# Routing of the last block: eight tiles in the first slot table, one operation at a time over slots 1 to 6, logits in plain float32

## The chip, the core and the metric

The kernel runs on one core of a Trainium2 chip. The metric is the time on the device in microseconds (us), the median of a few runs. The engines meant here are TensorE (PE in the rows, its weight loads PEld), VectorE (DVE), ScalarE (ACT), GpSimd (POOL) and SyncE (SP), which issues most transfers. Each engine works through its own queue in order.

## What is computed

Three stages follow each other: windowed attention, a dense layer with a leaky activation, and a layer of eight experts in which each token goes to the one expert with the largest logit.

```python
# attention: batch 4, 8 heads, 576 tokens, head size 64, causal window of 64
attn = softmax(where(mask, q @ k.T / 8, -1e9)) @ v          # 2304 tokens x 512
h = attn @ w_in                                            # 512 x 2048
x = (maximum(h, 0) + alpha * minimum(h, 0)) @ w_out        # 2304 x 512
logits = x @ w_gate                                        # 512 x 8
expert_idx = argmax(logits, axis=1)
gate_w = softmax(logits)[arange(N), expert_idx]
for e in range(8):                                         # w1: 512 x 1024, w2: 1024 x 512
    mask = expert_idx == e
    out[mask] = gate_w[mask, None] * (maximum(x[mask] @ w1[e], 0) @ w2[e])
```

Large products run as three products of rounded halves ("fp32r"): high by high, low by high and high by low. The high half is a rounded copy, made on ScalarE; the low half is the rest, made by a subtraction on VectorE. Weights and activations are both split in this way.

## The kernel before

The 2,304 tokens are 18 tiles of 128 and five blocks of 4, 4, 4, 3 and 3 tiles. Attention and dense layer run block by block. The routing of a block begins when its dense output (`stage`) is there: logits, then `r_gate` (largest logit, the softmax weight, the one-hot of the expert), `r_rank` (nine small matmuls that count the tokens of each expert before each token), `r_place` (row and column of each token in a list of 128 x 152 entries, eight experts by tiles of 128), `r_onehot` (two one-hot matrices A and B for each tile), `r_list` (a matmul of A by B) and `r_add` (their sum into the list `lst`). For the first three blocks the logits are VectorE dot products (`r_dot`), also for the fourth. For the last block they go over TensorE: `r_trans` transposes a tile of `stage` and splits it into halves (a copy on ScalarE, a subtraction on VectorE, L454 and L455), and `r_logits` multiplies both halves by the split gate weights `wgc` (eight matmuls of 16 or 8 columns, L463 and L464, then a copy of 8 columns on ScalarE and an addition on VectorE).

The expert layer runs in slots. A slot is one tile of 128 tokens of one expert. `slot_table` computes from the list which expert and which tile each slot has. The first table (part 0) is made once the first four blocks are routed; it gives `K1` slots, filled with whole tiles of the first 1,920 tokens. The second (part 1) gives the rest, after the last block's routing. Of 25 possible slots 21 run with these inputs (504 matmuls of L743, 24 in a slot).

In `slot(s)`, in the order of the code: `e1` (24 matmuls, the first expert matrix), `htr` twice (transposes of the hidden layer, with a copy on ScalarE and the subtraction L730 on VectorE), `e2mm` (24 matmuls, the second expert matrix), `xtr` (transpose of the next slot's gathered tokens, with the subtraction L703), `gather(s + 2)` (index from list and table on VectorE, L684 to L689, then an indirect transfer by GpSimd). At eight places `step(i)` puts in one split of the next slot's weights (`split2`: the copy L819 on ScalarE, the subtraction L825 on VectorE), and at the odd ones `sregs` and `reload` on SyncE, which loads the weights for slot s + 2 if its expert is another than that of the slot before (1 MB for each of four pieces).

The order inside the slots is written out by hand (`manual_schedule`): each engine gets its instructions in the order of the code. `extra` names what of the last block's routing is put ahead of the split at which step. Before, that is: in slot 0 the transposes and logits of the three tiles and `r_gate`, in slot 1 `r_rank`, `r_place` and the first one-hots, in slot 2 the list and the first part of the second table (`table_step`), in slot 3 the rest. The block before slot 0, where the last dense block and the first table overlap, is ordered by a scheduler.

Of the kernel before, what the change touches and what calls it, by code (L numbers as in the profile page):

```python
# [7 lines left out]
FP32 = mybir.dt.float32  # L8
# [9 lines left out]
NE = 8  # L18
NSLOT = 25
K1 = 6  # L20
# [60 lines left out]
def attn_moe_moe_kernel(  # L81
# [55 lines left out]
    wgc = const.tile([128, 4, 2 * NE], FP32R, name="wgc")  # L137
# [310 lines left out]
    def r_trans(j, t, tag="xs"):  # L448
        b = rbank(j).rearrange("p (k c) -> p k c", k=4)
        for k in range(4):  # L450
            PE.transpose(b[:, k, :], stage[j][:, t, k * 128:k * 128 + 128], ident)
        th = spare(tag + "h")
        tl = spare(tag + "l")
        ACT.copy(out=th, in_=b)  # L454
        DVE.tensor_tensor(out=tl, in0=b, in1=f32(th), op=ALU.subtract)  # L455
        x1t[j, t] = (th, tl)

    def r_logits(j, t):
        th, tl = x1t.pop((j, t))
        n = BLOCKS[j][1]  # L460
# [27 lines left out]
    def r_gate(j):  # L488
# [10 lines left out]
        DVE.tensor_tensor(out=ls, in0=lg, in1=mb, op=ALU.subtract)  # L499
        ACT.activation(out=ls, in_=ls, func=ACTF.Exp)  # L500
        eq = small("eq", [NE])
        DVE.tensor_tensor(out=eq, in0=lg, in1=mb, op=ALU.is_equal)
        DVE.tensor_tensor(out=eq, in0=eq, in1=desc8.unsqueeze(1).to_broadcast([128, n, NE]), op=ALU.mult)
        mx = small("mx", [])
        DVE.tensor_reduce(out=mx, in_=eq, axis=AX.X, op=ALU.max)
        oh = small("oh", [NE], BF16)
        DVE.tensor_tensor(out=oh, in0=eq, in1=mx.unsqueeze(2).to_broadcast([128, n, NE]), op=ALU.is_equal)
        ss = small("gs", [])
        DVE.tensor_reduce(out=ss, in_=ls, axis=AX.X, op=ALU.add)
        DVE.tensor_scalar(out=ss, in0=ss, scalar1=1e-9, scalar2=None, op0=ALU.add)  # L510
        DVE.reciprocal(out=stage[j][:, 0:n, 512:XW], in_=ss.unsqueeze(2).to_broadcast([128, n, XW - 512]))
        s = stage.pop(j)
# [17 lines left out]
    def r_place(j):  # L530
# [20 lines left out]
        jf = small("gs", [])
        DVE.tensor_copy(out=jf, in_=ji)
        cf = small("cf", [])
        DVE.tensor_scalar(out=cf, in0=mx, scalar1=-float(NTILE), scalar2=float(NE * NTILE), op0=ALU.mult, op1=ALU.add)
        DVE.tensor_tensor(out=cf, in0=cf, in1=jf, op=ALU.add)
        for u in range(n):
            DVE.tensor_tensor(out=ohsum, in0=ohsum, in1=oh[:, u, :], op=ALU.add)
        rc[j] = (cf, pf)

    def r_onehot(j, h=0):  # L560
# [3 lines left out]
        for t in range(2 * h, min(2 * h + 2, n)):  # L564
# [36 lines left out]
    def slot_table(part):  # L601
# [9 lines left out]
        PE.matmul(out=b[:, 0:NE], lhsT=one16, rhs=ohsum, start=True, stop=True)  # L611
        ni = small("ni", [NE], I32)
        DVE.tensor_scalar(out=ni, in0=b[:, 0:NE], scalar1=127.0 * part, scalar2=None, op0=ALU.add)
        DVE.tensor_scalar(out=ni, in0=ni, scalar1=7, scalar2=None, op0=ALU.logical_shift_right)
        nb = small("nb", [NE])
        DVE.tensor_copy(out=nb, in_=ni)
        give(("R", NB))
        yield
        if part:
            DVE.tensor_tensor(out=nb, in0=nb, in1=tab["done"], op=ALU.subtract)  # L620
# [47 lines left out]
    def table_step():  # L668
        next(gen1, None)
# [378 lines left out]
```

## Time and profile before

| what | us |
|---|---|
| median of three runs | 767.79 (767.28 to 767.81) |
| the profiled execution, its own time | 767.55 |
| its span, first to last instruction | 765.8 |
| TensorE busy in the span | 748.1 (98%) |
| VectorE busy | 609.0 (80%) |
| ScalarE busy | 456.3 (60%) |
| start of slot 0 | 485.31 |
| start of slot 1 | 505.29 |
| start of slot 5 | 560.68 |

A slot's start is the start of its first `e1` matmul. The time that a slot takes is best read as the distance between such starts; busy times say which engine fills it. A row of the timeline gives the start and the length of an instruction, or of several of one form in a row. Ends overlap with the next start, so what an operation costs its engine is the distance from its start to the next one's.

### The profile page before, as it was taken

The numbers are of one execution on the slowest core, as the hardware profiler recorded it, in microseconds if no ns is written. First come the engines' busy times: TensorE is split into PE (matmuls) and PEld (weight loads), VectorE is DVE, ScalarE is ACT, GpSimd is POOL, SyncE is SP. The second block draws the span as 40 slices with busy tenths as digits, with TensorE's granted clock in tenths as the row PEclk, the third lists the DMA queues.
The fourth block names the chain that finished last, engine by engine and source line by source line (L and its number), as shares of the span: only waits on it lengthen the run. The fifth ranks groups of instructions, "written<-read, shape, count | busy, mean of one in ns | idle before, by whom it ended". The sixth has DMA issues, their size and how long they took to land. (4 is left out here: it accounts for less than half of the span.)

```text
span 765.8 us, 12642 instructions
## 1 busy us (share of the span) xinstructions
PE 748.1 (98%) x4567; PEld 612.4 (80%) x4572; DVE 609.0 (80%) x1154; ACT 456.3 (60%) x868; POOL 89.4 (12%) x106
## 2 busy tenths in 40 slices
PE   7999999999999999999999999999999999999996
PEld 3688888888888888888888988777788888888884
DVE  4999999477556756668775956699999999999997
ACT  4887565543243342344342323778889999889986
POOL 1210001000000000000000001011222213131322
PEclk9999999999999999999999999999999999999999
DMA  9983413233032122223323116420194176757611
GB/s 347 411 363 131 157 64 120 68 103 105 24 94 97 62 62 98 62 98 90 93 66 111 56 43 268 161 109 28 56 353 169 32 279 258 290 214 258 215 73 51
DMA packets 29442, 109.90 MB, mean 144 GB/s; under 512 B 3582, under 2 KB 3966, under 8 KB 22208
## 3 DMA queue, kind: packets, MB, share of 16 engines
q1 hardware_dynamic: 25856, 98.25, 36.0%
q0 software_dynamic: 3520, 10.80, 4.3%
q8 instruction: 38, 0.62, 0.3%
q14 instruction: 28, 0.23, 0.1%
HBM read 154.09 MB, written 10.26 MB: 215 GB/s over the span
## 5 line engine op out<-in xcount | busy, mean ns | idle before, releaser
L825 DVE TENSOR_TENSOR hl<-hl,hl 128x1024 fp32r<-128x1024 f32 x176 | 211.1, 1222 | 17.7 <-ACT hl L819 17.0
L819 ACT CAST hl<-hl 128x1024 fp32r<-128x1024 f32 x176 | 180.4, 1049 | 6.0 <-DMA hl<-in_wx_dram 4.5
L743 PE MATMUL acc<-hl,xl 128*128 128x512 f32 x504 | 130.6, 400 | 2.5 <-DVE xl L730 2.5
L404 ACT ACTIVATE g<-h 128x512 f32<-128x512 f32 (+1 forms) x80 | 44.6, 558 | 141.2 <-PE h L391 110.9
L389 PE MATMUL h<-xh,hl 128*128 128x512 f32 (+1 forms) x320 | 120.6, 377 | 0.8 <-DVE g L408 0.8
L390 PE MATMUL h<-xl,hl 128*128 128x512 f32 (+1 forms) x320 | 118.1, 369 | 0.0
L391 PE MATMUL h<-xh,hl 128*128 128x512 f32 (+1 forms) x320 | 118.0, 369 | 0.0
L432 PE MATMUL acc<-hl,gl 128*128 128x512 f32 x288 | 113.2, 393 | 0.4 <-DVE gl L414 0.4
L433 PE MATMUL acc<-hl,gh 128*128 128x512 f32 x288 | 112.6, 391 | 0.0
L431 PE MATMUL acc<-hl,gh 128*128 128x512 f32 x288 | 109.9, 400 | 0.0
L743 PEld LDWEIGHTS acc<-hl,xl 128*128 128x128 f32 x504 | 91.2, 188 | 21.4 <-DVE xl L730 3.8
L408 DVE SCALAR_TENSOR_TENSOR g<-g,beta,h 128x512 f32<-128x512 f32 (+1 forms) x80 | 55.3, 691 | 56.0 <-ACT g L404 55.7
L414 DVE TENSOR_TENSOR gl<-g,gh 128x512 fp32r<-128x512 f32 (+1 forms) x80 | 50.8, 634 | 36.9 <-PE acc L432 22.2
L349 ACT CAST gh<-g 128x512 fp32r<-128x512 f32 (+1 forms) x80 | 46.5, 581 | 51.9 <-DVE g L408 50.2
L691 POOL DMA_INDIRECT gx<-x1d,ixg x23 | 39.9, 1733 | 290.3 <-DVE xh L703 166.6
L389 PEld LDWEIGHTS h<-xh,hl 128*128 128x128 f32 x320 | 60.1, 188 | 11.0 <-DVE g L408 1.3
L715 PE MATMUL h<-hl,xh 128*128 128x512 f32 x168 | 67.7, 403 | 0.0
L485 DVE SCALAR_TENSOR_TENSOR dot<-stage,wge 128x512 bf16<-128x512 f32 x96 | 65.8, 686 | 2.1 <-DMA wge<-in_wgt_dram 0.8
L390 PEld LDWEIGHTS h<-xl,hl 128*128 128x128 f32 x320 | 60.2, 188 | 8.6 <-DVE xl L377 0.5
L717 PE MATMUL h<-hl,xh 128*128 128x512 f32 x168 | 66.2, 394 | 0.4 <-DVE xh L703 0.2
L391 PEld LDWEIGHTS h<-xh,hl 128*128 128x128 f32 x320 | 60.1, 188 | 7.9
L716 PE MATMUL h<-hl,xh 128*128 128x512 f32 x168 | 65.5, 390 | 0.0
(194 smaller groups left out, 1071.8 us busy)
## 6 DMA issues: line engine op xcount, KB each, us to landing
hl<-in_wx_dram SPq DMA_DIRECT2D x92, 1024.0 KB
hl<-in_wcat_dram SPq DMA_DIRECT2D x14, 1024.0 KB
qk<-in_qkv_dram SPq DMA_DIRECT2D x30, 448.0 KB
v<-in_qkv_dram SPq DMA_DIRECT2D x30, 256.0 KB
wge<-in_wgt_dram SPq DMA_DIRECT2D x24, 256.0 KB
x1d<-stage SPq DMA_DIRECT2D x3, 1032.0 KB
hl<-in_qkv_dram SPq DMA_DIRECT2D x6, 448.0 KB
x<-in_wcat_dram SPq DMA_DIRECT2D x2, 1024.0 KB
```

The lines of the kernel that those rows point to most:

```text
L389: PE.matmul(out=h[:, 0:n], lhsT=w_in_op(f, k, 0), rhs=xh[:, k, :], start=(k == 0), stop=False)
L390: PE.matmul(out=h[:, 0:n], lhsT=w_in_op(f, k, 0), rhs=xl[:, k, :], start=False, stop=False)
L391: PE.matmul(out=h[:, 0:n], lhsT=w_in_op(f, k, 1), rhs=xh[:, k, :], start=False, stop=(k == 3))
L431: PE.matmul(out=a, lhsT=gh[:, c0:c0 + 128], rhs=w_out_op(f, 0), start=(f == 0), stop=False)
L432: PE.matmul(out=a, lhsT=gl[:, c0:c0 + 128], rhs=w_out_op(f, 0), start=False, stop=False)
L433: PE.matmul(out=a, lhsT=gh[:, c0:c0 + 128], rhs=w_out_op(f, 1), start=False, stop=(f == 15))
L485: DVE.scalar_tensor_tensor(out=o, in0=stage[j][:, t, 0:512], scalar=1.0, in1=wge[j, e], op0=ALU.mult, op1=ALU.mult, accum_out=rt[j][:, t, ...
L715: PE.matmul(out=o, lhsT=th[:, k, :], rhs=wh, start=(k == 0), stop=False)
L717: PE.matmul(out=o, lhsT=tl[:, k, :], rhs=wh, start=False, stop=(k == 3))
L743: PE.matmul(out=o, lhsT=x[:, f % 4, :], rhs=w[:, lo, (f % 2) * 512:(f % 2) * 512 + 512], start=(x is th and f == 0 and lo == 0), stop=(x i ...
L819: ACT.copy(out=t[:, 0, :], in_=r)
L825: eng.tensor_tensor(out=t[:, 1, :], in0=r, in1=f32(t[:, 0, :]), op=ALU.subtract)
```

## The change

`K1` goes from 6 to 8: the first table has eight slots, the second at most 17. The logits of the last block are computed from one plain float32 copy of the transposed tile: four float32 products of eight columns for a tile, then `r_take` copies the result; the halves, `wgc`, and the small copy and addition go. The first tile's transposes and logits stay in slot 0, those of the second and third go to slot 1. The functions of the routing become generators that yield after each VectorE operation; `route_last` strings them together with pauses of three steps ahead of what TensorE has to deliver, and `tick` takes one or two steps of it at each split from the sixth of slot 1 on (`PACE`), and one more at four places of slots 2 to 6. For the other blocks `drain` runs the same functions in one go.

```diff
-K1 = 6
+K1 = 8
@@ r_trans, r_logits
-        th = spare(tag + "h")
-        tl = spare(tag + "l")
-        ACT.copy(out=th, in_=b)
-        DVE.tensor_tensor(out=tl, in0=b, in1=f32(th), op=ALU.subtract)
-        x1t[j, t] = (th, tl)
+        x1t[j, t] = mp.tile([128, 128 * NBT], FP32, tag="g", bufs=1, name="g").rearrange("p (k c) -> p k c", k=4)
+        ACT.copy(out=x1t[j, t], in_=b)
...
-            PE.matmul(out=b[:, 0:2 * NE], lhsT=th[:, k, :], rhs=wgc[:, k, :], start=(k == 0), stop=False)
-            PE.matmul(out=b[:, 0:NE], lhsT=tl[:, k, :], rhs=wgc[:, k, 0:NE], start=False, stop=(k == 3))
-        lo = rp.tile([128, NE], FP32, tag="lo", name="lo")
-        ACT.copy(out=lo, in_=b[:, NE:2 * NE])
-        DVE.tensor_tensor(out=rt[j][:, t, :], in0=b[:, 0:NE], in1=lo, op=ALU.add)
+            PE.matmul(out=b[:, 0:NE], lhsT=x[:, k, :], rhs=wg[:, k * NE:k * NE + NE], start=(k == 0), stop=(k == 3))
+        x1t[j, t] = b
+
+    def r_take(j, t):
+        DVE.tensor_copy(out=rt[j][:, t, :], in_=x1t.pop((j, t))[:, 0:NE])
@@ r_gate, r_place, r_onehot, slot_table: after each VectorE operation
+        yield
...
+    WAIT = 3
...
+    def route_last():
+        j = NB - 1
+        yield from r_gate(j)
+        yield from pause()
+        r_rank(j)
+        yield from pause()
+        yield from r_place(j)
+        yield from r_onehot(j)
+        yield from pause()
+        r_list(j)
+        yield from r_onehot(j, 1)
+        r_add(j)
+        yield from pause()
+        r_list(j, 1)
+        yield from pause()
+        r_add(j)
+        yield from pause()
+        yield from slot_table(1)
...
+    routing = route_last()
+    PACE = {}
+    for _s in range(1, K1):
+        for _i in range(8):
+            if (1, 4) < (_s, _i) < (K1 - 2, 4):
+                PACE[_s, _i] = 1 + _i % 2
+
+    def tick(n):
+        for _ in range(n):
+            next(routing, None)
@@ slot
-            0: {0: [(r_trans, NB - 1, 0)], 1: [(r_trans, NB - 1, 1, "ht")], 2: [(r_logits, NB - 1, 0)],
-                3: [(r_trans, NB - 1, 2), (r_logits, NB - 1, 1)], 4: [(r_logits, NB - 1, 2)], 7: [(r_gate, NB - 1)]},
-            1: {1: [(r_rank, NB - 1), (r_place, NB - 1)], 6: [(r_onehot, NB - 1)]},
-            2: {0: [(r_list, NB - 1), (r_add, NB - 1)], 1: [(r_onehot, NB - 1, 1)], 2: [(r_list, NB - 1, 1), (r_add, NB - 1)], 4: [(table_step,), (table_step,)]},
-            3: {i: [(table_step,)] for i in (0, 2, 4, 6)},
+            0: {0: [(r_trans, L, 0)], 2: [(r_logits, L, 0)], 4: [(r_take, L, 0)]},
+            1: {0: [(r_trans, L, 1)], 2: [(r_logits, L, 1), (r_trans, L, 2)], 4: [(r_take, L, 1), (r_logits, L, 2)],
+                5: [(r_take, L, 2)]},
...
                 split2(s + 1, i)
+                tick(PACE.get((s, i), 0))
...
+        more = int(1 < s < K1 - 1)
```

How this moves instructions shows on two engines. On VectorE in slot 1 of the kernel before, the gate of the last block (L496 to L511, from the logits `lg` to the weight in `stage`) stands in one piece between two splits (L825):

```order
L825 TENSOR_TENSOR hl_4806<-hl_4697,hl_4806 128x1024
L496 TENSOR_REDUCE m<-lg 128x3
L499 TENSOR_TENSOR ls<-lg,m 128x24
L502 TENSOR_TENSOR eq<-lg,m 128x24
L503 TENSOR_TENSOR eq<-eq,c 128x24
L505 TENSOR_REDUCE mx<-eq 128x3
L507 TENSOR_TENSOR oh<-eq,mx 128x24
L509 TENSOR_REDUCE gs<-ls 128x3
L510 TENSOR_SCALAR gs<-gs 128x3
L511 RECIPROCAL stage<-gs 128x3x4
L825 TENSOR_TENSOR hl_4838<-hl_4697,hl_4838 128x1024
```

In the changed kernel the same gate (now L488 to L511) begins at the end of slot 1, with one or two operations between splits (now L895):

```order
L895 TENSOR_TENSOR hl_4977<-hl_4692,hl_4977 128x1024
L488 TENSOR_REDUCE m<-lg 128x3
L492 TENSOR_TENSOR ls<-lg,m 128x24
L895 TENSOR_TENSOR hl_5017<-hl_4694,hl_5017 128x1024
L496 TENSOR_TENSOR eq<-lg,m 128x24
L895 TENSOR_TENSOR hl_5027<-hl_4694,hl_5027 128x1024
L498 TENSOR_TENSOR eq<-eq,c 128x24
L501 TENSOR_REDUCE mx<-eq 128x3
L895 TENSOR_TENSOR hl_4739<-hl_4688,hl_4739 128x1024
L504 TENSOR_TENSOR oh<-eq,mx 128x24
L895 TENSOR_TENSOR hl_4771<-hl_4688,hl_4771 128x1024
```

Eight operations that stood in a row now stand among five splits. On TensorE in slot 0 before, the first tile's logits (L463 and L464) stand between the first hidden transpose (L726) and the last piece of the first expert matrix (L715):

```order
L726 MATMUL att_67<-c,hr 128x128 x4
L463 MATMUL att_68<-wgc,xh 128x16
L464 MATMUL att_68<-wgc,xh 128x8
L463 MATMUL att_68<-wgc,xh 128x16
L464 MATMUL att_68<-wgc,xh 128x8
L463 MATMUL att_68<-wgc,xh 128x16
L464 MATMUL att_68<-wgc,xh 128x8
L463 MATMUL att_68<-wgc,xh 128x16
L464 MATMUL att_68<-wgc,xh 128x8
L715 MATMUL h<-hl_4838,xh 128x512
```

In the changed kernel, in slot 1, the second tile's logits (L455) and the third tile's transposes (L447) stand at that place:

```order
L787 MATMUL h<-hl_5017,xh 128x512
L796 MATMUL att_68<-c,hr 128x128 x4
L455 MATMUL acc_5006<-c,g 128x8 x4
L447 MATMUL att_67<-c,stage 128x128 x4
L785 MATMUL h<-hl_5027,xh 128x512
```

The eight small products of halves are four plain ones, and two of the three tiles have moved a slot later.

## Rows read from the trace of the kernel before

**Rows 1.** Windows by slot, 0 to 5 and 15: length, then busy time (count).

```profile
core 0: us, PE busy (x) PEld busy (x) DVE busy (x) ACT busy (x) POOL busy (x), PEclk, DMA share, GB/s
485.31:505.29 19.98, 19.60 (x106) 15.39 (x105) 15.26 (x24) 15.19 (x24) 0.94 (x1) 1.00 0.29 106
505.29:519.66 14.37, 12.91 (x70) 10.18 (x69) 13.90 (x37) 11.11 (x15) 1.87 (x2) 1.00 0.27 94
519.66:533.57 13.91, 13.25 (x65) 10.64 (x64) 13.31 (x29) 11.21 (x14) 1.23 (x2) 1.00 0.13 38
533.57:546.73 13.16, 12.88 (x61) 10.03 (x60) 12.99 (x25) 11.10 (x14) 3.89 (x2) 1.00 0.14 41
546.73:560.68 13.95, 12.87 (x61) 10.03 (x60) 13.81 (x24) 11.11 (x14) 3.26 (x3) 1.00 0.49 165
560.68:572.98 12.30, 12.30 (x61) 10.18 (x60) 11.70 (x16) 11.12 (x14) 2.90 (x3) 1.00 0.95 362
683.79:696.47 12.68, 12.62 (x61) 10.10 (x60) 12.56 (x18) 11.81 (x15) 4.24 (x3) 1.00 0.53 176
```

**Rows 2.** TensorE's waits from 480 us on: us in total, times, longest.

```profile
PE acc L743 <- DVE xl L730: 2.5, 3, 1.5
```

**Rows 3.** Timeline of VectorE, slots 0 and 1: start, length, instruction.

```profile
496.85 0.15 DVE L467 TENSOR_TENSOR lg<-att,lo 128x8 f32<-128x8 f32 x1
496.93 1.21 DVE L825 TENSOR_TENSOR hl<-hl,hl 128x1024 fp32r<-128x1024 f32 x1
...
506.58 0.17 DVE L496 TENSOR_REDUCE m<-lg 128x3 f32<-128x24 f32 x1
506.79 0.18 DVE L499 TENSOR_TENSOR ls<-lg,m 128x24 f32<-128x24 f32 x1
506.89 0.18 DVE L502 TENSOR_TENSOR eq<-lg,m 128x24 f32<-128x24 f32 x1
...
508.20 2.36 DVE L825 TENSOR_TENSOR hl<-hl,hl 128x1024 fp32r<-128x1024 f32 x2
510.48 0.18 DVE L539 TENSOR_TENSOR ls<-att,oh 128x24 f32<-128x24 f32 x1
...
512.21 1.22 DVE L825 TENSOR_TENSOR hl<-hl,hl 128x1024 fp32r<-128x1024 f32 x1
```

**Rows 4.** Timeline of VectorE, the second table's first and last stretch.

```profile
530.67 0.16 DVE L613 TENSOR_SCALAR ni<-att 128x8 int32<-128x8 f32 x1
...
531.87 1.22 DVE L825 TENSOR_TENSOR hl<-hl,hl 128x1024 fp32r<-128x1024 f32 x1
...
548.55 0.17 DVE L650 SCALAR_TENSOR_TENSOR col<-es,jn 128x19 f32<-128x19 f32 x1
...
549.78 4.67 DVE L825 TENSOR_TENSOR hl<-hl,hl 128x1024 fp32r<-128x1024 f32 x4
```

**Rows 5.** Timeline of VectorE, end of slot 9: gather index, then the input's subtraction.

```profile
620.58 0.37 DVE L684 SCALAR_TENSOR_TENSOR scr<-c,col,lst 128x152 f32<-128x152 f32 x1
...
621.12 0.68 DVE L703 TENSOR_TENSOR xh<-att,xh 128x512 fp32r<-128x512 f32 x1
621.72 1.22 DVE L825 TENSOR_TENSOR hl<-hl,hl 128x1024 fp32r<-128x1024 f32 x1
```

**Rows 6.** Timeline of TensorE in slot 0.

```profile
493.60 0.66 PE L726 MATMUL att<-c,hr 128*128 128x128 f32 x4
494.01 0.26 PE L463 MATMUL att<-wgc,xh 128*128 128x16 f32 x1
...
494.90 0.48 PE L715 MATMUL h<-hl,xh 128*128 128x512 f32 x1
...
502.46 3.00 PE L743 MATMUL acc<-hl,xl 128*128 128x512 f32 x12
```

**Rows 7.** TensorE's weight loads, 493 to 495 us: busy us, mean ns, idle before.

```profile
L464 PEld LDWEIGHTS att<-wgc,xh 128*128 128x128 f32 x4 | 0.8, 192 | 0.0
...
L726 PEld LDWEIGHTS att<-c,hr 128*128 128x128 f32 x4 | 0.4, 140 | 0.4 <-ACT hr L720 0.4
```

**Rows 8.** ScalarE's waits from 560 us on.

```profile
ACT hl L819 <- DMA hl<-in_wx_dram: 1.0, 1, 1.0
```

More of the change, by code (lines that the diff above doesn't have):

```diff
@@ L611, in slot_table @@
         PE.matmul(out=b[:, 0:NE], lhsT=one16, rhs=ohsum, start=True, stop=True)
+        for _ in range(WAIT * part):
+            yield
         ni = small("ni", [NE], I32)
         DVE.tensor_scalar(out=ni, in0=b[:, 0:NE], scalar1=127.0 * part, scalar2=None, op0=ALU.add)
+        yield
         DVE.tensor_scalar(out=ni, in0=ni, scalar1=7, scalar2=None, op0=ALU.logical_shift_right)
+        yield
         nb = small("nb", [NE])
         DVE.tensor_copy(out=nb, in_=ni)
+        yield
         give(("R", NB))
-        yield
         if part:
             DVE.tensor_tensor(out=nb, in0=nb, in1=tab["done"], op=ALU.subtract)
+            yield
         t8 = small("t8", [NE, NE])
         DVE.tensor_tensor(out=t8, in0=le8, in1=nb.unsqueeze(1).to_broadcast([128, NE, NE]), op=ALU.mult)
+        yield
         cum = small("cum", [NE])
@@ L633, in slot_table @@
         DVE.tensor_scalar(out=ec, in0=es, scalar1=float(NE - 1), scalar2=None, op0=ALU.min)
+        yield
         ctl = small("ctl", [2, ns], I32)
         DVE.tensor_copy(out=ctl[:, 0, :], in_=ec)
+        yield
         DVE.tensor_tensor(out=ctl[:, 1, 1:ns], in0=ec[:, 1:ns], in1=ec[:, 0:ns - 1], op=ALU.not_equal)
+        yield
         if part:
             DVE.tensor_tensor(out=ctl[:, 1, 0:1], in0=ec[:, 0:1], in1=tab["last"], op=ALU.not_equal)
+            yield
             tot = small("tot", [1], I32)
             DVE.tensor_copy(out=tot, in_=cum[:, NE - 1:NE])
+            yield
             tab["tot"] = tot
         tab["ctl", part] = ctl
+        DVE.tensor_tensor(out=cmp, in0=cmp, in1=nb.unsqueeze(1).to_broadcast([128, ns, NE]), op=ALU.mult)
         yield
-        DVE.tensor_tensor(out=cmp, in0=cmp, in1=nb.unsqueeze(1).to_broadcast([128, ns, NE]), op=ALU.mult)
         jn = small("jn", [ns])
         DVE.tensor_reduce(out=jn, in_=cmp, axis=AX.X, op=ALU.add)
+        yield
         DVE.tensor_tensor(out=jn, in0=siota[:, 0:ns], in1=jn, op=ALU.subtract)
@@ L659, in slot_table @@
             DVE.tensor_tensor(out=done, in0=nb, in1=cum, op=ALU.subtract)
+            yield
             DVE.tensor_scalar(out=done, in0=done, scalar1=float(K1), scalar2=0.0, op0=ALU.add, op1=ALU.max)
+            yield
             DVE.tensor_tensor(out=done, in0=done, in1=nb, op=ALU.min)
+            yield
             tab["done"] = done
@@ L665, in slot_table, with drain, pause @@
         tab["col", part] = col
-        yield
-    def table_step():
-        next(gen1, None)
+    WAIT = 3
+    def drain(g):
+        for _ in g:
+            pass
+    def route_last():
[16 more added lines that the diff above has]
+        yield from slot_table(1)
+    def pause():
+        for _ in range(WAIT):
+            yield
+    routing = route_last()
[7 more added lines that the diff above has]
+            next(routing, None)
     def where(s):
@@ L873, in attn_moe_moe_kernel @@
             at(last + 2 + e // 2, 5, r_dot, NB - 2, e * BLOCKS[NB - 2][1] + t)
-    at(last + 6, 6, r_gate, NB - 2)
+    at(last + 6, 6, lambda: drain(r_gate(NB - 2)))
     at(last + 7, 6, r_rank, NB - 2)
-    at(last + 7, 6, r_place, NB - 2)
-    at(last + 7, 6, r_onehot, NB - 2)
+    at(last + 7, 6, lambda: drain(r_place(NB - 2)))
+    at(last + 7, 6, lambda: drain(r_onehot(NB - 2)))
     at(last + 8, 0, r_list, NB - 2)
     at(last + 8, 0, r_add, NB - 2)
-    at(last + 8, 0, r_onehot, NB - 2, 1)
+    at(last + 8, 0, lambda: drain(r_onehot(NB - 2, 1)))
     at(last + 9, 0, r_list, NB - 2, 1)
     at(last + 9, 0, r_add, NB - 2)
-    at(last + 9, 6, lambda: [None for _ in slot_table(0)])
+    at(last + 9, 6, lambda: drain(slot_table(0)))
     at(last + 9, 6, sregs, 0)
@@ L936, in slot @@
         htr(s, 0)
+        tick(more)
         step(2)
@@ L941, in slot @@
         htr(s, 1)
+        tick(more)
         step(4)
@@ L944, in slot @@
             gather(s + 2)
+        tick(more)
         e2mm(s, 1)
@@ L947, in slot @@
             xtr(s + 1)
+        tick(more)
         step(5)
```

40 lines of the change are left out of this document (31 added, 9 removed).

## The prediction

> **What bounds the kernel now.** I read the busy shares first (TensorE busy almost throughout), then the windows by slot, because the change touches only the last stage, the 21 slots of the second expert layer. There the windows show two regimes [rows 1]. From slot 5 on a slot takes 12.30 us, TensorE is busy in all of it, and VectorE in 11.70. In slots 1 to 4 a slot takes 14.37, 13.91, 13.16 and 13.95 us, with TensorE idle in part and VectorE full up to 0.1 to 0.6 us: there VectorE sets the pace. The waits say the same: TensorE waits for the lower halves that VectorE writes at L730 [rows 2]. The granted clock is 1.00 in all of them, so the clock is no matter here.
>
> What fills VectorE in slots 1 to 4 is the routing of the last block: chains of tiny operations. In the timeline a dependent one starts 0.21 us after the one before it (506.58 to 506.79), an independent one 0.10 us after (506.79 to 506.89), and one that stands alone in front of a large operation costs 0.08 us (496.85 to 496.93) [rows 3]. The gate's nine operations take 1.62 us (506.58 to 508.20), the twelve of the placing 1.73 us (510.48 to 512.21) [rows 3]; the slot table's five stretches take from 1.20 us (the first) to 1.23 us (the last), with 0.57, 0.51 and 0.79 between them, 4.30 us in all [rows 4]. With about 1.85 us for the three one-hot pairs and two list additions, which the change only moves, that is 9.5 us of VectorE time in four slots.
>
> What VectorE can spare is little. Its own work in a slot is eight splits at 1.14 us (508.20 to 510.48, two of them) [rows 3], three subtractions at 0.60 and a gather's index at 0.54 us [rows 5]: 11.43 us, so 0.87 us are free of 12.30. Four slots give 3.5 us to 9.5 us of extra work; the rest, less the lead that VectorE has at the end of slot 0, is what slots 1 to 4 lost: 55.39 us in sum [rows 1], against 4 x 12.30 plus about 0.8 us of routing matmuls, so 5.4 us lost.
>
> **The change, part by part.** All sums are against the profiled execution, 767.55 us with a span of 765.8; the median of the runs, 767.79, lies 0.24 above, and I add that at the end.
>
> *Slots 0 and 1: two tiles' transposes and logits move from slot 0 to slot 1.* TensorE sets both slots. In slot 0 the first transpose of the hidden layer starts at 493.60 after a wait for ScalarE's ReLU [rows 6, 7]; ScalarE's order up to there doesn't change, so 493.60 stays, and the removal of the transposes in front of it gives nothing. From there to the end of slot 0 were 11.69 us. Of these go the third tile's transposes (0.41, as the four from 493.60 to 494.01), two logits (0.89 each, as the first tile's from 494.01 to 494.90) [rows 6] and 0.3 us of switches and waits around them (an estimate). What they take in plain float32 the trace doesn't show. Now eight products with eight or sixteen columns start 0.11 us apart, as fast as their weight loads, which take 192 ns; the load of a plain float32 tile of 128 x 128 takes 140 ns in the transposes [rows 7]. With eight loads a tile as now I take 0.89 x 140/192 = 0.65 us. The bounds: 0.4 us, half of what eight records at the transposes' pace would take, and 1.8 us if a product leaves twice as many records at 0.11. Slot 0 becomes 8.29 + 11.69 - 0.41 - 2 x 0.89 - 0.3 - 0.24 = 17.25 us. Slot 1 is 12.30 plus two tiles' transposes (0.41 each) and two logits (0.65 each): 14.4 us. VectorE's load there is its 11.43 and 0.9, so it doesn't bind. Together 31.65 against 34.35 us: **2.7 us won**. Most of it is slot 1, where gate and placing held up TensorE (14.37 us [rows 1]) and now aren't done yet.
>
> The Trainium skill (FP8 and Floating Point Precision, TensorE Precision Notes) says that true FP32 takes four passes through the array. No run here shows this for eight columns; if that means four loads for each product, a tile has sixteen, 1.3 us at 140/192 of 0.11, and the sum would be 2 us worse.
>
> *VectorE loses three subtractions (0.60 each) and three additions, ScalarE three small copies; three copies of the logits come.* All of it in slots 0 and 1, beside TensorE: nothing, and 1.8 us if TensorE didn't cover it.
>
> *Routing one operation at a time, over slots 1 to 6.* In the new order each step stands between splits, at most two side by side. By the spacings above a lone small operation costs 0.08 to 0.10 and a pair 0.31 us; those of 64 elements 0.14, of 136 elements 0.22. Counted along the order: gate 1.28 (1.62 before), placing 1.31 (1.73), table 3.38 (4.30), one-hots and list 1.85 as before: 7.82 us, 1.67 us less. Where they fall matters as much. TensorE takes three results of VectorE in a slot: the lower half of the first hidden transpose, after five splits and a subtraction (6.28 us), that of the second, after two and one (2.87), and that of the next slot's input, after one split, the gather and a subtraction (2.28). At TensorE's pace of 0.23 to 0.24 us for a matmul (502.46, twelve of them to 505.29) [rows 6] it asks for them 6.29, 3.46 and 2.55 us apart. So there is no slack at all ahead of the first, 0.6 us ahead of the second and 0.27 ahead of the third, and VectorE leads by at most some 0.4, 0.65 and 0.9 us there (estimates, from the steady slots). The extras that the new order puts ahead of the three are: slot 2: 1.20, 0.16, 0; slot 3: 1.04, 0.54, 0.67; slot 4: 0.69, 0.22, 0; slot 5: 1.45, 0.34, 0.52; slot 6: 1.07. Carried along with the leads, the loss is 0 in slot 2, 0.1 and 0.35 in slot 3, 0.25 in slot 4, 0.75 in slot 5 and 1.05 in slot 6: 2.5 us. The same bookkeeping gives 4.7 for before where 5.4 were lost, so I take 2.5 x 5.4/4.7 = 2.9. Slots 2 to 6 become 5 x 12.30 + 0.7 of routing matmuls + 2.9 = 65.1 us; before, 13.91 + 13.16 + 13.95 + 2 x 12.30 = 65.6: **0.5 us won**. The bounds are 1.5 us lost (the small operations go into VectorE's waits for ScalarE) and 5.4 us (as before).
>
> By the Trainium skill (VectorE: DVE Perf Modes, The DRAIN you can't avoid) the next operation doesn't start until the pipe is empty, a semaphore costs nothing extra, and what counts is the number of operations. The trace disagrees for 24 elements: 0.21 us with a dependence, 0.10 without [rows 3].
>
> *Eight slots in the first table.* The first 1,920 tokens fill 12 tiles of 128 by expert (from the reference's inputs), so eight are there, and 21 slots remain. Experts change at slots 1, 8, 9 instead of 1, 6, 7: as many loads, two slots later. Loads of neighbouring changes come just in time: once ScalarE waited 1.0 us for one [rows 8], and slot 15 took 12.68 us [rows 1]. If VectorE's delay in slot 6 does that to slots 8 and 9, it costs 0.4 us; I take 0.
>
> *SyncE.* The store of the last block's rows, with its wait for the gate's reciprocal, moves from slot 0 to slot 2 in SyncE's queue. Behind it stand loads that aren't taken while expert 1 goes on (to slot 6), and the first gather that needs these rows comes in slot 6: nothing. Two conversions of the gate weights near the start go, in front of a wait of VectorE for TensorE: nothing.
>
> Sum: 2.7 + 0.5 = 3.2 us, 764.4 for the profiled execution and **764.6 us** against the median.
>
> **The rivals.** (1) *A lone operation costs what it costs in the chain*, 0.21 us, since the pipe empties anyway. Then VectorE saves no 1.67 us, and the time is 766.3. For it: in before nearly no small one stands alone; against it: those that do (496.85) cost 0.08. This is the skill's rule above. (2) *The lumps stay*: slots 5 and 6 have 2.3 and 1.1 us of extras, more than any slack, and lose what slots 1 to 4 lost (5.4): 767.1. For it: the pair and the reductions ahead of the first result, where there is no slack; against it: 1.67 us less of work and five slots. (3) *Slower: plain float32 is dear on TensorE.* A tile's logits with sixteen loads of 192 ns that nothing covers take 3.1 us; TensorE sets slots 0 and 1, so three tiles cost 3 x (3.1 - 0.65) = 7.3 us: 771.9. It loses over 0.2% from 2.2 us a tile on. Against it: today's eight loads of 192 ns take 0.89 us, so they overlap. At 1.8 us a tile it would be 768.0. (4) *More is won*: the extras go into VectorE's waits (1.5 us lost) and logits take 0.4 us: 762.5.
>
> **How the numbers follow.** A run of this kernel can tell 0.2% (1.5 us) from no change: faster is under 766.3, slower over 769.3. Forecast 0.55 (763.6 to 766.0); rival 1 0.14 and rival 2 0.09 (766.3 to 767.1); rival 3 0.06 at 768.0 and 0.05 at 771.9; rival 4 0.11. Faster: the forecast, rival 4 and half of rival 1, 0.73; slower 0.05 and a little for what I don't see, 0.07; same 0.20. The range leaves out rival 3 and the far part of rival 4: 762.6 to 767.2.
>
> **What would show it.** Slots 0 and 1 of 17.25 and 14.4 us, a tile's logits of 0.65 us, small operations with 0.08 to 0.10 us to the next split, slots 2 to 6 at 65 us with the loss in slots 5 and 6, and slots 7 on at 12.30. Wrong would be logits over 1 us, small operations at 0.2 us between splits, or slots 2 to 4 still at 13.5 us and more.

## The result

The changed kernel takes **771.66 us** (median of 5 runs, 770.41 to 772.13) against 767.28 for the kernel before (766.46 to 767.81): a ratio of **1.0054**, with a 95% interval of 1.0039 to 1.0069. It is slower by some 4 us. The forecast was 764.6 us, the range 762.6 to 767.2; both missed, and the sign too.

The windows by slot of the changed kernel, to be laid beside [rows 1]: slots 0 to 7, then 15 (length, then busy time and count of each engine; PEclk is TensorE's granted clock, 1.00 being 2.4 GHz and 0.50 being 1.2 GHz).

```profile
core 0: us, PE busy (x) PEld busy (x) DVE busy (x) ACT busy (x) POOL busy (x), PEclk, DMA share, GB/s
484.60:502.07 17.47, 16.71 (x82) 12.79 (x81) 12.81 (x19) 13.83 (x19) 0.85 (x1) 1.00 0.33 121
502.07:522.33 20.26, 18.41 (x86) 15.31 (x85) 13.68 (x21) 12.37 (x17) 2.60 (x3) 0.83 0.14 40
522.33:534.98 12.65, 12.65 (x71) 10.44 (x70) 11.35 (x23) 11.10 (x14) 1.62 (x2) 1.00 0.22 84
534.98:548.98 14.00, 12.77 (x64) 10.34 (x63) 13.86 (x31) 11.11 (x14) 3.51 (x3) 1.00 0.13 39
548.98:563.74 14.76, 12.95 (x63) 10.31 (x62) 12.71 (x20) 11.11 (x14) 1.99 (x2) 1.00 0.12 38
563.74:576.34 12.60, 12.60 (x62) 10.10 (x61) 12.34 (x30) 11.13 (x14) 1.38 (x1) 1.00 0.12 41
576.34:589.65 13.31, 12.63 (x62) 10.04 (x60) 13.24 (x23) 11.11 (x14) 2.38 (x3) 1.00 0.50 174
589.65:601.96 12.31, 12.31 (x61) 10.19 (x60) 11.66 (x16) 11.11 (x14) 2.87 (x3) 1.00 0.92 360
...
688.19:701.09 12.90, 12.61 (x62) 10.10 (x60) 12.77 (x20) 11.87 (x15) 4.24 (x3) 1.00 0.51 170
```

Read down the first column. Slot 0 is 2.51 us shorter than before, as meant. Slot 1 is 5.89 us longer (20.26 against 14.37), and in this one slot the clock stands at 0.83 and not at 1.00. Slots 2 to 6 sum to 67.32 against 65.62 us, 1.70 longer. In slot 4 VectorE is busy for 12.71 of 14.76 us only: it isn't the engine that sets the pace there. With 0.22 in slot 15 and a stage that starts 0.71 us earlier, this makes 4.59 us, against 4.58 between the two profiled executions (772.13 and 767.55). The last two terms vary from run to run: take_early and fill (below), with the instructions of the changed kernel ahead of slot 1, start slot 0 at 485.17 and 485.76 us and take 13.09 and 12.83 us in slot 15.

**Slot 1.** TensorE's waits from 484 to 602 us name what is new (us in total, times, longest); before, only the last kind of product, the lower half's, had a long one there [rows 2].

```profile
PE acc L455 <- DVE lg L459: 1.9, 1, 1.9
PE att L624 <- DVE lst L597: 1.4, 1, 1.4
PE acc L592 <- DVE B L581: 1.2, 1, 1.2
PE acc L813 <- DVE xl L800: 0.7, 1, 0.7
PE att L592 <- DVE B L581: 0.5, 1, 0.5
```

L455 are the plain float32 logits, L459 the small copy that empties their bank. The timelines of TensorE and of VectorE around it (start, length, instruction, wait before it):

```profile
507.06 0.96 PE L455 MATMUL acc<-c,g 128*128 128x8 f32 x8
507.87 0.64 PE L447 MATMUL att<-c,stage 128*128 128x128 f32 x4
...
511.10 0.60 PE L796 MATMUL att<-c,hr 128*128 128x128 f32 x4
513.55 1.47 PE L455 MATMUL acc<-c,g 128*128 128x8 f32 x8 [1.85 <-DVE lg L459]
514.87 2.91 PE L813 MATMUL acc<-hl,xl 128*128 128x512 f32 x6
```

```profile
511.59 1.23 DVE L895 TENSOR_TENSOR hl<-hl,hl 128x1024 fp32r<-128x1024 f32 x1 [0.20 <-ACT hl L889]
512.74 0.68 DVE L800 TENSOR_TENSOR xl<-att,xl 128x512 fp32r<-128x512 f32 x1
513.34 0.16 DVE L459 COPY lg<-acc 128x8 f32<-128x8 f32 x1
```

The second tile's logits were done at 507.87, but the copy of them stands in VectorE's queue behind the subtraction of the second hidden transpose (L800), which itself needs TensorE's transposes of 511.10, by way of ScalarE's copy of them (511.74 to 512.33); the split ahead of the subtraction, which ends later than that copy, adds some 0.4 us. The third tile's logits take the same bank ("acc"), and wait. Then the clock falls: two windows, the wait, and 6.82 us at half the clock that begin 0.49 us after the restart.

```profile
511.46:513.55 2.09, 0.24 (x3) 0.00 (x1) 1.96 (x4) 1.63 (x3) 0.00 (x0) 1.00 0.00 0
514.04:520.86 6.82, 6.82 (x22) 5.65 (x22) 2.49 (x8) 2.19 (x3) 0.98 (x1) 0.50 0.16 41
```

The eight records of logits, 0.81 us at 507.06, now take 1.32 us (513.55 to 514.87), the later part of them at half the clock; six products of the second layer, 1.53 us at 509.74, take 2.91.

### The profile page after: what moved, and what is told of

The parts are those of the page before. It is cut to its first block, busy times and chain, and to the rows that moved or that the text cites. A ratio compares the mean times of both kernels' runs of the same rounds, so it can differ in the third digit from the quotient of the medians.

```text
span 770.4 us, 12635 instructions
## 1 busy us (share of the span) xinstructions
PE 750.1 (97%) x4572; PEld 614.2 (80%) x4572; DVE 606.0 (79%) x1149; ACT 455.6 (59%) x865; POOL 84.5 (11%) x106
## 4 chain that ended last, share of the span: by engine, by line
PE 82%; DVE 6%; DMA 5%; ACT 3%; issue 2%; SPq 1%; POOL 0%; ACTq 0%; POOLq 0%
PE acc L813 12%; PE acc L427 8%; PE h L385 8%; PE acc L428 8%; PE h L386 8%; PE acc L429 8%; PE h L387 8%; PE h L787 4%; DVE hl L895 4%; PE h L785 4%; PE h L786 4%; DMA hl<-in_wcat_dram 3%; PE att L360 2%; DMA hl<-in_wx_dram 2%; PE att L291 2%
## 5 line engine op out<-in xcount | busy, mean ns | idle before, releaser
L895 DVE TENSOR_TENSOR hl<-hl,hl 128x1024 fp32r<-128x1024 f32 x176 | 211.8, 1222 | 21.4 <-ACT hl L889 20.6
L813 PE MATMUL acc<-hl,xl 128*128 128x512 f32 x504 | 133.1, 406 | 0.7 <-DVE xl L800 0.7
L813 PEld LDWEIGHTS acc<-hl,xl 128*128 128x128 f32 x504 | 92.8, 192 | 21.6 <-DVE xl L800 1.7
L761 POOL DMA_INDIRECT gx<-x1d,ixg x23 | 37.2, 1618 | 289.9 <-DVE xh L773 127.2
```

The costliest lines, as they stand in the source:

```text
L813: PE.matmul(out=o, lhsT=x[:, f % 4, :], rhs=w[:, lo, (f % 2) * 512:(f % 2) * 512 + 512], start=(x is th and f == 0 and lo == 0), stop=(x i ...
L895: eng.tensor_tensor(out=t[:, 1, :], in0=r, in1=f32(t[:, 0, :]), op=ALU.subtract)
```

## The experiments

Two theories stood at the start. **W:** the wait for the copy, and the clock that falls with it, are the loss of slot 1. **F:** the form is, short plain float32 products, wait or no wait. All ratios below are to the kernel before, whose median beside them was 766.7 to 767.3 us.

| run | median us | ratio, 95% interval |
|---|---|---|
| take_early | 766.96 | 1.0004 (0.9994 to 1.0014) |
| fill | 772.20 | 1.0063 (1.0047 to 1.0080) |
| before_k8 | 767.00 | 1.0001 (0.9992 to 1.0011) |
| before_plain | 765.88 | 0.9993 (0.9983 to 1.0002) |
| fill2 | 768.33 | 1.0024 (1.0014 to 1.0035) |
| lists_late | 764.26 | 0.9969 (0.9960 to 0.9978) |
| k12 | 764.63 | 0.9973 (0.9961 to 0.9985) |
| lumps | 766.97 | 1.0004 (0.9994 to 1.0014) |
| early | 764.87 | 0.9971 (0.9959 to 0.9984) |
| early_exp | 763.29 | 0.9950 (0.9937 to 0.9964) |
| early_even | 762.92 | 0.9948 (0.9935 to 0.9962) |

**take_early: the copy one step earlier.**

```diff
-            1: {0: [(r_trans, L, 1)], 2: [(r_logits, L, 1), (r_trans, L, 2)], 4: [(r_take, L, 1), (r_logits, L, 2)],
+            1: {0: [(r_trans, L, 1)], 2: [(r_logits, L, 1), (r_trans, L, 2)], 3: [(r_take, L, 1)], 4: [(r_logits, L, 2)],
```

> The changed kernel, with the copy of the second tile's logits (the 24-element VectorE copy that empties the bank) issued one step earlier, ahead of the subtraction of the second hidden transpose. Theory W (the wait): slot 1 took 20.25 us because the third tile's logits waited 1.85 us for that copy, and TensorE's granted clock then fell to 0.5 for 6.83 us. Without the wait the clock stays at 1.00, slot 1 takes 14.4 to 15.0 us, the other slots stay, and the time is 771.7 - 5.5 = 766.2 us (765.8 to 766.8). Rival F (the form): the plain float32 logits themselves, short products of eight columns, bring the clock down or cost the time, wait or no wait: slot 1 stays over 17.5 us with a granted clock under 1.00, and the time is 769 us or more.

Slots 1, 3 and 4 in its windows:

```profile
502.66:517.69 15.03, 15.03 (x85) 12.78 (x84) 12.60 (x18) 12.15 (x16) 2.61 (x3) 1.00 0.13 39
...
530.80:544.80 14.00, 12.80 (x63) 10.36 (x62) 13.82 (x31) 11.11 (x14) 3.48 (x3) 1.00 0.12 39
544.80:559.58 14.78, 12.97 (x64) 10.31 (x63) 12.71 (x20) 11.12 (x14) 2.00 (x2) 1.00 0.13 38
```

Slot 1 falls from 20.26 to 15.03 us at a clock of 1.00 with the same plain float32 logits in it. F is out. The time is that of the kernel before, not less, and just above the expected range: slots 2 to 6 are still long, 67.80 us in sum, and slot 2, expected to stay at 12.65 us, takes 13.11.

**fill and fill2: the wait filled with work.** Nine products that nobody uses, ahead of the third tile's logits:

```diff
+        for _ in range(9):
+            PE.matmul(out=b, lhsT=hT[1, 0][0][:, 0, :], rhs=ring[1, 4][:, 0, 0:512], start=True, stop=True)
```

> The changed kernel, with nine matmuls of 128x512 (0.228 us each, 2.05 us in sum, into a bank that is free there) put on TensorE in front of the third tile's logits; their result is overwritten and used by nobody. They stand where TensorE idled for 2.1 us, so the wait is no shorter, only filled. Theory W, in its part on the clock: with TensorE busy the clock stays at 1.00, slot 1 takes 20.25 - 3.5 = 16.7 us and the time is 768.2 us (767.8 to 768.6): 2.1 us of the loss are the wait, some 3.5 the clock. Rival F: the clock falls all the same, slot 1 stays at 20.2 us or more, 771.7 us. Third case, the filler lengthens the slot because the wait is shorter than it looks: slot 1 at 17.5 us with the clock at 1.00.

This run missed its aim: I had given the filler the bank that the logits were to get, so it waited for the copy itself (its own row, first below). Its slot 1 (20.70 us) and its time are those that rival F names, but they say nothing for it, since the wait is still there. The second try took the bank that the third tile's transposes had left.

> The changed kernel with the nine matmuls of 128x512 put in front of the third tile's logits once more, now into the bank that the third tile's transposes left, which is free before the wait begins (in the run before they had the bank of the logits and waited themselves). Theory W on the clock: TensorE works through the 2.1 us in which it idled, the granted clock stays at 1.00, slot 1 takes 15.0 + 2.1 = 17.1 us against 20.25, and the time is 768.9 us (768.4 to 769.4). Rival: the clock falls with something else there (the logits, the transposes): granted clock under 1.00 in slot 1, slot 1 at 18.8 us or more, 770.5 us or more.

The filler's row in fill (timeline of TensorE) and a window behind its start, then the filler's row in fill2 and the window of slot 1 there:

```profile
514.73 3.71 PE L461 MATMUL acc<-hl,xl 128*128 128x512 f32 x9 [1.85 <-DVE lg L464]
```

```profile
515.30:518.60 3.30, 3.30 (x11) 2.65 (x9) 1.01 (x5) 0.00 (x0) 0.98 (x1) 0.50 0.16 37
```

```profile
511.32 2.31 PE L461 MATMUL att<-hl,xl 128*128 128x512 f32 x9
```

```profile
501.93:519.01 17.08, 17.08 (x94) 14.36 (x93) 12.62 (x18) 12.16 (x16) 2.59 (x3) 1.00 0.16 48
```

In fill the wait is there, and the clock falls again, here for 3.3 us, with 128x512 products behind the wait in place of the logits. In fill2 TensorE works through the same stretch, and the clock stays at 1.00. Slot 1 takes 17.08 us, 17.1 were expected; the time, 768.33, is just under its range. The third tile's logits start 11.54 us into the slot, in the changed kernel 11.48, so the filler takes up the stretch of the wait and no more. That splits the loss: 17.08 - 15.03 = **2.05 us are the wait** and 20.26 - 17.08 = **3.2 us the clock** after it.

**before_k8 and before_plain: two parts of the change alone.** The first sets K1 to 8 in the kernel before. The second puts plain float32 logits in the places of the split ones in slot 0:

```diff
-            PE.matmul(out=b[:, 0:2 * NE], lhsT=th[:, k, :], rhs=wgc[:, k, :], start=(k == 0), stop=False)
-            PE.matmul(out=b[:, 0:NE], lhsT=tl[:, k, :], rhs=wgc[:, k, 0:NE], start=False, stop=(k == 3))
+            PE.matmul(out=b[:, 0:NE], lhsT=x[:, k, :], rhs=wg[:, k * NE:k * NE + NE], start=(k == 0), stop=(k == 3))
```

> The kernel before with one number changed: a first table of eight slots instead of six, its routing and its split logits where they were. Theory W counts the table's size at nothing: slots 1 to 4 as before (14.4, 13.9, 13.2, 13.9 us), the change of expert after the first table at slots 8 and 9 instead of 6 and 7, 767.3 us plus or minus 0.4. Rival L (loads): the weight loads of the neighbouring changes now come two slots later and late; slots 8 and 9 over 12.6 us, or slot 15 over 12.7, and 768 us or more.

> The kernel before with the three tiles' logits in plain float32, at the places where the split ones stood in slot 0, and the transposed rows in tiles of their own. Theory W: 0.81 us a tile (read in the changed kernel) against 0.89 us: 0.2 us less on TensorE in slot 0, and three subtractions (0.60) and three additions less on VectorE ahead of the gate; slot 0 at 19.2 to 19.8 us, clock 1.00, 766.9 us (766.3 to 767.4). Rival F: plain float32 is dear or brings the clock down: slot 0 over 20.5 us or a granted clock under 1.00 in slots 0 and 1, 768 us or more.

before_k8 did what was expected: slots 8 and 9 take 12.34 and 12.30 us, and slot 15, at 12.73, is within 0.05 us of before; a table of eight slots costs nothing that shows. In before_plain slot 0 takes 19.84 us against 19.98, clock 1.00, and slots 1 to 4 are those of before. Its time is 0.4 us under the expected range, but in its trace slots 0 to 8 are only 0.14 us shorter than before; the rest lies outside them: slot 0 starts earlier (483.70) and slot 15 is shorter (12.36). Neither part is behind the loss, and neither alone can be told from no change.

**lumps: the new places of the logits, the routing unspread.** take_early with gate, placing, lists and table in stretches as before, one slot later:

```diff
+                5: [(r_take, L, 2)], 7: [(lambda: drain(r_gate(L)),)]},
+            2: {1: [(r_rank, L), (lambda: drain(r_place(L)),)], 6: [(lambda: drain(r_onehot(L)),)]},
+            3: {0: [(r_list, L), (r_add, L)], 1: [(lambda: drain(r_onehot(L, 1)),)], 2: [(r_list, L, 1), (r_add, L)],
+                4: [(table, 6)]},
+            4: {0: [(table, 2)], 2: [(table, 5)], 4: [(table, 3)], 6: [(table, 6)]},
```

> take_early with the routing in lumps, as the kernel before had it, one slot later: gate at the end of slot 1, rank and place after the second split of slot 2, one-hots after the seventh, lists at the start of slot 3, the slot table in five stretches in slots 3 and 4. Theory C: spreading alone bought nothing, since what it saved VectorE was lost in waits: slots 2 to 5 take 14.4, 13.9, 13.2 and 13.9 us as slots 1 to 4 did before, slot 6 12.30, 67.7 us in sum, 766.9 us (766.3 to 767.4). Rival S: spreading itself costs (a lone operation is dearer than in a chain): the lumps are faster by over 1 us, 765.9 us or less. Rival G: spreading is worth its 1.7 us: 768.4 us or more.

Slots 2 to 6 sum to 67.57 us against 67.80 in take_early, and the times are the same: spreading bought nothing here. It did save work. The pages' first rows of lumps and of take_early, which differ in nothing else, have VectorE at 607.1 and 605.6 us, 1.5 us less:

```profile
PE 747.9 (98%) x4572; PEld 612.3 (80%) x4572; DVE 607.1 (79%) x1149; ACT 455.7 (60%) x865; POOL 90.7 (12%) x106
```

```profile
PE 747.6 (97%) x4572; PEld 612.6 (80%) x4572; DVE 605.6 (79%) x1149; ACT 455.6 (59%) x865; POOL 87.0 (11%) x106
```

**lists_late: three products of the routing later.** The saved work went into waits: in slots 2 to 6 VectorE waits 2.8 us for ScalarE in take_early and 1.1 us in lumps, and TensorE 3.8 us for VectorE against 3.0. In take_early TensorE stands in front of the list's products (L592) and the table's (L624) as in the changed kernel. The rows around the first two of them, from the timeline of all engines:

```profile
542.87 0.28 DVE L581 TENSOR_SCALAR B<-c,pf 128x128 fp32r<-128x128 f32 x1
543.20 0.34 PE L592 MATMUL acc<-A,B 128*128 128x152 f32 x1 [1.20 <-DVE B L581]
545.00 0.69 ACT L819 ACTIVATE gx<-acc,gx 128x512 f32<-128x512 f32 x1 [1.96 <-PE acc L813]
545.59 1.99 ACT L889 CAST hl<-hl 128x1024 fp32r<-128x1024 f32 x2
...
546.67 1.23 DVE L895 TENSOR_TENSOR hl<-hl,hl 128x1024 fp32r<-128x1024 f32 x1 [0.36 <-ACT hl L889]
...
548.14 0.34 PE L592 MATMUL att<-A,B 128*128 128x152 f32 x1 [0.45 <-DVE B L581]
...
550.39 0.59 ACT L799 CAST xl<-att 128x512 fp32r<-128x512 f32 x1 [1.05 <-PE att L796]
...
551.01 0.69 DVE L800 TENSOR_TENSOR xl<-att,xl 128x512 fp32r<-128x512 f32 x1 [0.42 <-ACT xl L799]
```

That is a circle: TensorE waits for VectorE's one-hot, ScalarE for TensorE's products (with its copies for the next slot queued behind), VectorE for ScalarE's copies. The edit lengthens three pauses, and lets the steps go on for one split more in slot 6 (`PACE`):

```diff
         yield from r_onehot(j)
-        yield from pause()
+        yield from pause(6)
         r_list(j)
...
-        yield from pause()
+        yield from pause(6)
         r_list(j, 1)
...
-        yield from pause()
+        yield from pause(5)
         yield from slot_table(1)
...
-            if (1, 4) < (_s, _i) < (K1 - 2, 4):
+            if (1, 4) < (_s, _i) < (K1 - 2, 5):
```

> take_early, with the two products of the list and the ones product of the slot table put 3, 3 and 2 places later in the order, and what follows them with them. Theory C (a circle of queues): in slots 3 and 4 TensorE stood 1.2, 0.45 and 1.36 us in front of these three products, ScalarE's ReLUs and copies came late for it, and VectorE idled 1.9 us for ScalarE's copies. Without these waits slots 2 to 6 come near VectorE's own work of 64.5 us: 65.3 us against 67.8, and the time is 764.5 us (763.9 to 765.3). Rival V: VectorE's work alone sets these slots, and the waits only move to the lower halves (the subtraction's products): slots 2 to 6 stay over 67 us, 766.3 us or more.

Slots 2 to 6 take 64.81 us, 3.0 less than in take_early, and the time is 764.26; slots 3 and 4:

```profile
530.97:543.29 12.32, 12.32 (x62) 10.13 (x60) 12.16 (x30) 11.12 (x14) 2.53 (x2) 1.00 0.15 44
543.29:556.63 13.34, 13.18 (x64) 10.36 (x63) 13.31 (x21) 11.11 (x14) 3.42 (x3) 1.00 0.13 40
```

VectorE's waits for ScalarE in slots 2 to 6 are 1.2 us now, and none of the three waits is left; these are all of TensorE's from 485 to 602 us:

```profile
PE acc L813 <- DVE xl L800: 1.1, 2, 0.9
PE acc L796 <- ACT hr L790: 0.4, 1, 0.4
PE acc L428 <- DVE gl L410: 0.4, 1, 0.4
```

Rival V is out: the waits did not move to the lower halves, which have 1.1 us now against 0.8.

**k12: twelve slots, one step a split.**

```diff
-K1 = 8
+K1 = 12
...
-                PACE[_s, _i] = 1 + _i % 2
+                PACE[_s, _i] = 1
```

> take_early with a first table of twelve slots and one routing step behind each of the eight splits of slots 2 to 10, no further ones. Theory: VectorE has 0.87 us free in a slot, and eight lone small operations take 0.65 to 0.9 us, so nearly nothing is lost but the routing's products: slots 2 to 11 take 124.5 us against 129.3 us in take_early, and the time is 762.2 us (761.6 to 764.0). Rival L: the first table's twelve slots go through more changes of expert, and the loads come late: slots over 13 us, 766 us or more. Rival C: the three products still stand in front of VectorE's results and TensorE waits for them over 1 us in sum: 764 to 766 us.

764.63 us: better than before, 2.4 short of what was expected. Two new waits are the likely reasons, each a row (TensorE's and ScalarE's); no run took either of them away. Rival L was in part right; rival C's time came, but by another product than its three.

```profile
PE att L769 <- DVE ls L540: 1.6, 1, 1.6
```

```profile
ACT hl L889 <- DMA hl<-in_wx_dram: 1.7, 2, 1.4
```

The first is a bank again: the ranks' bank is freed by the first step of the placing, which the slower pace put so late that the next slot's transposes (L769) came first; slot 3 took 14.43 us. The second is the price of a larger table that before_k8 didn't have: the expert changes at slots 8, 9, 10 and 11 in a row (from the reference's inputs), ScalarE waited for their loads, and slot 10 took 13.78 us.

**early, early_exp, early_even: the logits back in slot 0, the routing from slot 1 on.** before_plain had shown that all three plain logits fit into slot 0 at 19.84 us, which leaves slots 1 to 6 for the routing.

> lists_late with all three tiles' plain float32 logits back in slot 0, where the kernel before had them (transposed rows in tiles of their own), and the routing's steps from the first split of slot 1 on. Theory (VectorE's work sets slots 1 to 6 once nobody waits for a product that stands too early): six slots of VectorE's own 11.43 us and 7.8 us of routing are 76.4 us, less a lead of some 1 us out of slot 0; slot 0 takes 19.8 us as in the run with plain logits alone, slots 1 to 6 75.4 to 76.4 us, slots 7 and 8 12.3 each, against 17.47 + 15.03 + 64.81 + 12.45 + 12.70 = 122.46 us in lists_late: 1.6 to 2.6 us less, 762.2 us (761.5 to 763.2). Rival C: moved by twelve steps, some product stands in front of VectorE's result again, and TensorE waits over 1 us in sum: 763.5 us or more. Rival L: the loads for slot 8 come late whatever VectorE does (0.9 us of ScalarE's wait in lists_late): 0.4 us of it stay.

764.87 us against 762.2 expected, nothing gained on lists_late: slot 1 took 13.20 us, where TensorE's own work is 12.3. ScalarE's exponential (L495) stood in its queue at the start of slot 1, ahead of what TensorE needs, and waited for VectorE's subtraction (ScalarE's waits, then TensorE's):

```profile
ACT ls L495 <- DVE ls L493: 1.4, 1, 1.4
```

```profile
PE acc L814 <- ACT xl L800: 0.6, 1, 0.6
```

```diff
         DVE.tensor_tensor(out=ls, in0=lg, in1=mb, op=ALU.subtract)
         yield
-        ACT.activation(out=ls, in_=ls, func=ACTF.Exp)
...
         DVE.tensor_tensor(out=eq, in0=eq, in1=desc8.unsqueeze(1).to_broadcast([128, n, NE]), op=ALU.mult)
         yield
+        ACT.activation(out=ls, in_=ls, func=ACTF.Exp)
```

> The run before (early) with one line moved: ScalarE's exponential of the gate two steps later in the order. There it stood in ScalarE's queue at the start of slot 1 in front of VectorE's subtraction, ScalarE waited 1.4 us for it with the first ReLU and copies behind, TensorE 0.6 us for the hidden transpose, and slot 1 took 13.20 us. If that is what kept the gain of early away: slot 1 at 12.3 to 12.5 us, 764.9 - 0.8 = 764.1 us (763.4 to 764.7). If VectorE's own work in slot 1 is the cause: slot 1 stays at 13 us, 764.9 us.

> The same with the steps laid out evenly: one behind each split and four in between in every slot from 1 to 6, two behind the eighth split only, and pauses of 5, 5 and 3 steps ahead of the three products. By VectorE's work alone slots 1 to 6 could take 75.5 us against 78.0 in early; a pair of dependent steps side by side costs 0.31 us, two lone ones 0.2, and some 16 pairs go: 1 to 1.5 us less than early_exp, 762.8 us (762.2 to 763.6). If TensorE then waits for one of the products, or the last steps of the table crowd slot 6 (13.56 us in early): no gain, 764 us.

Slot 1 of early_exp takes 12.32 us: the exponential was it. The time, 763.29, is just under its range; slots 0 to 8 are 0.94 us shorter than in early (121.59 and 122.53), 0.88 of it in slot 1, so what the medians differ by beyond that isn't shown to be its work. Laid out evenly the time is **762.92 us**, 0.9948 of the kernel before (0.9935 to 0.9962), the fastest of all. The interval of its gain on early_exp isn't clear of zero; the traces' slots 0 to 8 sum to 121.59 and 120.55 us. Slots 3 and 6 of early_even:

```profile
529.83:542.84 13.01, 12.84 (x64) 10.33 (x62) 12.97 (x24) 11.12 (x14) 3.35 (x3) 1.00 0.13 42
...
567.75:580.97 13.22, 12.57 (x61) 10.11 (x60) 13.15 (x26) 11.12 (x14) 3.24 (x3) 1.00 0.52 166
```

Of the 2.3 us that slots 1 to 6 still take over 12.30 each, 1.6 stand in these two, where VectorE is full.

## Why the prediction was wrong

**Slot 0, 17.25 us:** right, 17.47. Its mechanism, that only work behind the first hidden transpose counts, holds: that transpose starts 8.29 us into the slot in both kernels.

**Slot 1, 14.4 us: the step that failed.** It was worked out as a sum of TensorE's work, with "VectorE's load there is its 11.43 and 0.9, so it doesn't bind". The load indeed doesn't bind (12.60 of 15.03 us in take_early); the place of one copy in VectorE's queue does, one of the "three copies of the logits" that the prediction put at nothing. The step asked how much VectorE has to do in the slot, not what TensorE waits for and what stands ahead of that. The list of instructions had it: the third tile's logits and the second's use one bank, and the copy between them stands behind the subtraction that waits for the second hidden transpose. That cost 2.05 us, and the clock another 3.2, of which nothing was said, since "the granted clock is 1.00 in all of them, so the clock is no matter here" took the clock of the kernel before for that of the kernel after. take_early gives what slot 1 is without both: 15.03 us. Of the 0.6 above 14.4, 0.4 are the logits, which were mis-sized: 0.81 and 0.89 us a tile and not 0.65 (within the stated bounds of 0.4 to 1.8). Most of the rest are switches between kinds of products, of which the sum took 0.3 us out of slot 0 and put none into slot 1: the logits start 0.44 us after the hidden transposes there, where the next product otherwise follows after 0.36, and behind the second tile's transposes the first product takes 0.31 us to the next one and not 0.23.

On a bank that is shared the Trainium skill (Perfetto Trace Analysis, section Matmuls) says that independent groups of products should rotate through different banks, so that emptying one overlaps the next group's products. Here three banks did rotate, over transposes and logits alike, and the row of 1.85 us shows it isn't enough: what counts is whether the bank's last reader has had its turn in its own queue.

**Slots 2 to 6, 65.1 us:** the sum of the work was right, the waits were not. A lone small operation costs what was forecast, and a dependent one next to another what it cost before, as these rows of the changed kernel's VectorE show: 0.07 us from the lone L550 to the split, 0.20 from L544 to L547, which needs its result.

```profile
535.42 0.17 DVE L544 TENSOR_REDUCE m<-ls 128x3 f32<-128x24 f32 x1
535.62 0.17 DVE L547 CAST ri<-m 128x3 int32<-128x3 f32 x1
...
536.84 0.16 DVE L550 TENSOR_SCALAR pi<-ri 128x3 int32<-128x3 int32 x1
536.91 1.22 DVE L895 TENSOR_TENSOR hl<-hl,hl 128x1024 fp32r<-128x1024 f32 x1
```

With it rival 1, the lone operation at the chain's price, is out. The Trainium skill's rule that stood behind it (VectorE: DVE Perf Modes, The DRAIN you can't avoid), that the next operation does not start until the pipe is empty, is not what these rows show for a next operation without a dependence; the section itself says that one which is not held starts earlier. The 1.67 us of VectorE's work forecast as saved were 1.5 (lumps against take_early). But the bookkeeping of leads knew three results a slot that TensorE takes from VectorE, the lower halves; the routing itself has products that take VectorE's one-hots and its list, and the new order puts TensorE in front of three of them too early (1.4, 1.2 and 0.5 us). They are not in the sum. The trace of before had such a wait too, beside the one shown in [rows 2]:

```profile
PE att L579 <- DVE B L569: 0.5, 1, 0.5
```

The loss also fell elsewhere: forecast for slots 5 and 6 (0.75 and 1.05), it came in slots 3 and 4 (1.7 and 2.5 over 12.30); slot 6 was right (13.31), slot 5 not (12.60). Rival 2 had the size of this loss (5.4 us; 67.32 less five slots of 12.30 and 0.7 of routing products leaves 5.1), but put it into slots 5 and 6. With the three products later the five slots take 64.81 us, 0.3 under the forecast; slots 7 and 8 then take 12.44 and 12.71.

**Rival 3** named the measured time, 771.9, by another mechanism: sixteen records of 192 ns a tile. before_plain and take_early refute it. That plain float32 leaves twice the records of a product is so (x8 for four products), at 0.10 to 0.11 us each and not at 0.19; the Trainium skill's four passes (FP8 and Floating Point Precision, TensorE Precision Notes) are not seen in these records.

**Eight slots in the table, SyncE, ScalarE's and VectorE's work in slots 0 and 1 at nothing:** the first is shown by before_k8, but where the routing comes later the 0.4 us that the prediction named for late loads and took at 0 do come: in lists_late ScalarE waits 1.4 us for loads around slot 8, which takes 12.71 us and not 12.30. That the subtractions and additions that go give nothing is borne out by before_plain, with slots 1 to 4 unchanged; of the copies that come, one is the failed step. SyncE no run took apart. Slots 7 on at 12.30: right, but for slot 15. Two slips change nothing: VectorE's own work in a slot is 11.46 us by the terms given, not 11.43, and the gate that stands in one piece before has nine operations, not eight.

The two omissions are nearly the whole error: without the wait and the early products (lists_late) the change is at 764.26 us, 0.9969 of the kernel before; the forecast was 764.6 of 767.79, 0.9958.

## What to carry to other kernels

When an instruction that frees a bank or feeds TensorE is moved, look at what stands ahead of it in its own engine's queue, and at what that in turn waits for; an engine's free time in a stretch doesn't say that one operation of it comes in time. When work is spread thinly, count every result that another engine takes, those of the spread work itself too, and give the taker more distance, not less: three longer pauses were worth 3 us of 67.8 here. A wait on TensorE can bring the clock down behind it (3.2 us here after a wait of 2.05), and is to be priced with that.

## What was unexpected of the hardware

A wait of 1.85 us of TensorE, ahead of which stood 128x128 transposes and 128x512 products at a clock of 1.00, was followed by 6.8 us at 0.50 in the changed kernel and by 3.3 us in fill; it cost 3.2 us in the first, more than the wait. Waits of 1.23 and 1.36 us in slots 3 and 4 of the changed kernel, one of 1.58 us in slot 3 of k12 and one of 1.5 us before [rows 2] left the clock at 1.00 [rows 1].

The length of the wait alone doesn't decide it. Near the start of the executions TensorE waits for the first loads of the attention. In before it waited 2.52 us there and in k12 2.18 us, and the clock was 0.50 from 9 to 11 us; in early it waited 2.33 us, in fill 2.09, and the clock stayed at 1.00. What else decides it these runs don't show.
